# Two chunks of attention output, in two of four groups, turned by DMA instead of TensorE

## Chip, cores and metric

The kernel runs on one core of one Trainium2 chip. The metric is the device time of one execution in microseconds (us), taken as the median of several runs.

## What is computed

```python
xn = layernorm(x)                      # x: 1 x 2048 x 640, fp32
q, k, v = split(xn @ wqkv)             # 32 heads of 20
a = softmax over 8 keys at distance 0, 2, ..., 14 behind each token
s = (a applied to v) @ wo              # sliding dilated attention, then the output projection
h = silu(xn @ w1) @ w2                 # 640 -> 1536 -> 640
out = x + s * silu(h)
```

## The kernel before

**Groups and phases.** The 2048 tokens are cut into four groups of 512 (two halves of the sequence, and in each the even and the odd tokens, so that a distance of 2 becomes 1). Each group runs two phases on TensorE: QKV (`qkv_phase`, four quarters `q` of eight heads, each 5 x 4 x 3 matmuls of 480 columns) and FFN (`ffn_phase`: twelve blocks of w1 in `up`, twelve of w2 in `down`, and the output projection `wo_phase` of the group before). fp32 is carried as two fp32r parts, a high and a low one, and each product is three matmuls (high x high, low x high, high x low). VectorE does the attention of a group (`score`, `weigh`, `total`, `value`) while TensorE is in the FFN of the same group and at the start of the next QKV. The result goes into `O` (tokens on partitions, 640 columns), quarter by quarter; some of the last additions are done by GpSimd (lines 772 and 774), the others by VectorE.

**Turning.** TensorE needs the channels on partitions, so `O` and the normalised `x` are turned in five chunks of 128 columns. On TensorE that is `split_t` (line 620): four transposes of 128 x 128 against an identity (line 626) into one of two PSUM banks `rot`, a copy by ScalarE to the high part (line 630) and a subtraction by VectorE for the low part (line 636). `o_chunk` does that for `O`, called from QKV of the next group at the five places of `O_AT` (line 946: after the weights of chunk 2 or 4 in quarter 1, 2 or 3). Most of `x` is turned by DMA instead (`X_DMA`, `turn_x`, line 651): ScalarE packs the fp32 values into two planes of 16 bits (line 656), SyncE issues one DMA transpose for each plane (line 660), ScalarE puts the planes together again (line 665) and copies the high part (line 670), and VectorE subtracts (line 671).

**Buffers.** `OH`/`OL` and `TH`/`TL` are the same storage, 16 columns apart: in a slot lies first the turned `x` of a group, and, once its last w1 block is done, the turned `O` of that group, which `wo_phase` of the next FFN reads. `KV[q]` holds keys and values of a quarter, with a halo that DMAs fill (lines 693, 703 and 705); its key half is scratch for `value` (`partial`). Weights go through a ring of seven buffers `WR`; from the second or third use on they are loaded again by GpSimd's DMA queue (line 562), one load each time TensorE frees a buffer.

**Order.** Nothing is issued in the order in which the Python code names it. Every operation is added to a planner (`Weave`) with an engine, a duration, keys that it reads and writes, a priority, perhaps an earliest time `at`; `order` simulates the engines and fixes one order for each, and `plan` adds edges that close gaps on TensorE in that simulation. On the chip each engine runs its list in order and waits at the head of it. A small `prio` goes first. `spans` are ranges of `O` or `XIN` that wait for one another even where their columns differ.

Of the kernel before, what the change touches and what calls it, by code (L numbers as in the profile page):

```python
# [10 lines left out]
U16 = mybir.dt.uint16  # L11
AF = mybir.ActivationFunctionType
# [3 lines left out]
P = 128  # L16
# [5 lines left out]
CQ = HQ * DH  # L22
J = 8
T = 4
TOK = T * P
# [28 lines left out]
CARRY_AT = 8.0  # L54
X_SINGLE = (1,2,)
X_DMA = {1: (0, 1, 2, 3, 4), 2: (2, 3, 4)}
X_BY = {1: 2, 3: 0, 4: 1}
SLOW, ISSUE, SUB_LATE = 8, 2.0, 3
PACE0, PACE = -20.0, 12.0
BACK = {1: 0.0, 2: 40.0}  # L60
# [260 lines left out]
def local_attention_silu_ffn(ctx: ExitStack, tc: tile.TileContext, x, wqkv, wo, w1, w2, out):  # L321
    nc = tc.nc
# [18 lines left out]
    NG = len(groups)  # L341
# [15 lines left out]
    TH = [sb.tile([P, DC * TOK + OAT], F32R, name="th0")]  # L357
# [4 lines left out]
    TL = tiles("tl", 2, [P, DC * TOK + 64], F32R)  # L362
    chunks = lambda tiles, at: [v[:, at:at + DC * TOK].rearrange("p (c n) -> p c n", c=DC) for v in tiles]
    OH, OL = chunks(TH, OAT), chunks(TL, OAT)
    TH, TL = chunks(TH, 0), chunks(TL, 0)
# [6 lines left out]
    KV = tiles("kv", NQ, [P, 2, HALO + T, CQ])  # L372
    Q = tiles("q", NQ, [P, T, CQ])
    E = [v[:, :, CQ - W * HQ:].rearrange("p t (w h) -> p t w h", w=W) for v in Q]
    O = sb.tile([P, T, D], F32, name="o")
    PR = sb.tile([P, 2, W, CQ], F32, name="pr")
    L = tiles("l", 2, [P, T, W, HQ])
    XIN = sb.tile([P, T, D], F32, name="xin")
    G = sb.tile([P, T, D], F32, name="gate")
# [3 lines left out]
    TURN = sb.tile([P, TOK], F32, name="turn")  # L383
# [29 lines left out]
    def act(n, fn, reads, writes, prio, table=None, more=0.0, late=0.0, at=0.0, spans=()):  # L413
        return add("ACT", ac(n) + more, fn, reads, writes, prio, table=table, late=late, at=at, spans=spans)

    def free_for(old, new):

        add("DVE", 0.0, lambda: None, [], list(old) + list(new), 0)
# [8 lines left out]
    clock = [0.0]  # L427
# [214 lines left out]
    def both(k):  # L642
        return [k + (0,), k + (1,)]

    def chunk_span(of, c, write=False):
        return [(of, c * P, (T - 1) * D + (c + 1) * P, write)]

    def piece(tile_of, k):
        return tile_of.rearrange("p t d -> p (t d)")[:, k * TOK:(k + 1) * TOK]

    def turn_x(c, i, at, back):

        keys = [("xin", t) for t in range(T)]
        (a, ka), (b, kb) = (piece(G, X_BY[c]), ("buf", X_BY[c])) if c in X_BY else (TURN, ("turn",)), (piece(G, c), ("buf", c))
        into = XIN[:, :, c * P:(c + 1) * P]
        act(2 * TOK, lambda: nc.scalar.activation(
            a.bitcast(U16).rearrange("p (h t n) -> p h t n", h=2, t=T), into.bitcast(U16).rearrange("p t (n h) -> p h t n", h=2),
            AF.Copy), keys, both(ka), 150, at=at, spans=chunk_span("x", c))
        for h in range(2):
            dma(lambda h=h: nc.sync.dma_start_transpose(  # L660
                b.bitcast(U16).rearrange("p (h t n) -> p h t n", h=2, t=T)[:, h],
                a.bitcast(U16).rearrange("p (h n) -> p h n", h=2)[:, h]),
                [ka + (h,)], [kb + (h,)], P * TOK * 6, clock[0], ISSUE, SLOW)
        kh, kl = t_keys(i, [c], kinds=["th"]), t_keys(i, [c], kinds=["tl"])
        act(2 * TOK, lambda: nc.scalar.activation(
            into.bitcast(U16).rearrange("p t (n h) -> p h t n", h=2),
            b.bitcast(U16).rearrange("p (h t n) -> p h t n", h=2, t=T), AF.Copy),
            both(kb) + keys, [("xw", c)], 150, more=0.3, at=back, spans=chunk_span("x", c, True))
        hi, lo = (v[i][:, c, :].rearrange("p (t n) -> p t n", t=T) for v in (TH, TL))
        act(TOK, lambda: nc.scalar.activation(hi, into, AF.Copy), [("xw", c)] + keys, kh, 0)  # L670
        dve(TOK, lambda: nc.vector.tensor_tensor(out=lo, in0=into, in1=hi.bitcast(F32), op=OP.subtract),
            [("xw", c)] + keys + kh, kl, 0, lock=True, late=SUB_LATE, spans=chunk_span("x", c))

    def tile_spans(of, cs, ts):
        return [(of, t * D + c * P, t * D + (c + 1) * P, False) for t in ts for c in cs]
# [32 lines left out]
    def halo_keys(q):  # L708
        return [("halo", q, 1, 0), ("halo", q, 1, 112), ("halo", q, 2, 0), ("halo", q, 2, 112), ("halo", q, 3, 0),
                ("halo", q, 4, 0)] + [("kv", q, t) for t in range(T)]  # L710
# [93 lines left out]
    def o_chunk(g, c, i):  # L804
        qs = range(c * P // CQ, ((c + 1) * P - 1) // CQ + 1)
        split_t(O, [("o", q, t) for q in qs for t in (0, 2)], c, i, (OH, OL))
# [104 lines left out]
    def qkv_phase(g, i, io):  # L911
        for q in range(NQ):
            if g == 0 and q == 0:
                ps = first_quarter(i)
            else:
                ps = [bank() for t in range(T)]
                for c in range(DC):
                    wh, wl, kh, kl = w_next("q", q, c)
                    for t in range(T):
                        o, kp = ps[t]  # L920

                        def unit(c=c, t=t, o=trio_sums(o), wh=wh, wl=wl):
                            hi, lo = TH[i][:, c, tsl(t)], TL[i][:, c, tsl(t)]
                            vh, vl = trio(wh), trio(wl)
                            nc.tensor.matmul(o, hi, vh, start=c == 0, stop=False)  # L925
                            nc.tensor.matmul(o, lo, vh, start=False, stop=False)  # L926
                            nc.tensor.matmul(o, hi, vl, start=False, stop=c == DC - 1)  # L927
                        pe(3 * mm(3 * CQ), unit, t_keys(i, [c], [t]) + [kh, kl], [kp])
                    w_done()
                    if g:  # L930
                        for k in O_AT.get((q, c), ()):
                            o_chunk(g - 1, k, io)
            if groups[g][0] == 0:
                zero = KV[q][0:2, 0:2 - g, 0:HALO, :]
                add("POOL", 2.0 - g, lambda zero=zero: nc.gpsimd.memset(zero, 0.0), [] if g or not q else ["first"],
                    [("halo", q, 1, 0), ("halo", q, 2, 0), ("halo", q, 3, 0), ("halo", q, 4, 0)], clock[0] if g else 1 + 12 * q)
            for t in range(T):
                evac_qkv(g, q, t, *ps[t])
            halo(g, q)
            attend(g, q)  # L940
        attend(g, NQ)

    def t_keys(i, cs, ts=range(T), kinds=("th", "tl")):
        return [(k, i, c, t) for k in kinds for c in cs for t in ts]
# [37 lines left out]
    def gate(ts, cs):  # L982
        return of(G[:, ts.start] if ts.stop - ts.start == 1 else G[:, ts], cs)

    def gkeys(ts, cs):
        return [("g", t, cs.start) for t in range(ts.start, ts.stop)]
# [158 lines left out]
    def ffn_phase(g, i, ix, io):  # L1145
        if g + 1 < NG:
            behind = [("kv", XQ, 0)] if g else []
            step = 1 if g in X_SINGLE else 2
            for t in range(0, T, step):
                load_x(g + 1, t, step, behind=behind)  # L1150
            for t in range(T):
                ln_stats(t)
            ln_rstd(0, T)
            for t in range(T):
                ln_apply(t)
        ps = None
        by_dma = X_DMA.get(g, ())
        bufs = [("buf", c, h) for c in range(DC) for h in range(2)]
        for kind, f in plan(g):
            if kind == "w1":  # L1160
                up(g, i, f, io)
            elif kind == "wo":
                wo_phase(g - 1, io)
                if g == NG - 1:
                    free_for([("xin", t) for t in range(T)], [("xin", t, c) for t in range(T) for c in (0, CA)])
                for c in range(DC) if by_dma else ():
                    ts = slice(c * TOK // D, ((c + 1) * TOK - 1) // D + 1)
                    free_for(gkeys(ts, slice(0, CA)) + gkeys(ts, slice(CA, D)), bufs[2 * c:2 * c + 2])
                for k, c in enumerate(by_dma):
                    turn_x(c, ix, clock[0] + PACE0 + PACE * k, clock[0] + BACK[g])  # L1170
            elif kind == "x":
                if f not in by_dma:
                    split_t(XIN, [("xin", t) for t in range(T)], f, ix, (TH, TL), XIN[:, :, tsl(f)])
            elif kind == "o":
                o_chunk(g, f, io)
            elif kind == "rest":
                o_rest(g, f, io)
            else:
                ps = ps or tm_banks()
                down(f, ps)  # L1180
        for p, kp, ts, cs in tm_views(ps):
            n = (ts.stop - ts.start) * (cs.stop - cs.start)
            act(n, lambda p=p, ts=ts, cs=cs: nc.scalar.activation(gate(ts, cs), p, AF.Silu), [kp], gkeys(ts, cs) + bufs * bool(by_dma), 0, "silu")

    add("POOL", 0.7, consts, [], ["consts"], 0)
    act(1, lambda: nc.scalar.activation(SD[:, 1, 0:1], epst, AF.Sqrt), ["consts"], [("rs", 0)], 0, "sqrt")
# [37 lines left out]
```

## Time and profile before

| what | value |
|---|---|
| time, median of 3 runs (lowest, highest) | 602.38 us (601.88, 603.2) |
| the profiled execution | 600.52 us |
| its span, first to last instruction | 598.7 us |
| TensorE busy | 593.2 us, 99% |
| VectorE, ScalarE, GpSimd busy | 515.6, 236.9 and 163.5 us |
| granted TensorE clock, mean | 1.000 |

A matmul's duration in the profile runs from its start to its modelled end, and the next one starts before that end; so durations of TensorE add up to more than the busy time. The chain of waits that ended last shows each piece only for the time by which it moved the end. QKV of the four groups starts at about 7, 139, 284 and 431 us.

### The profile page before, as it was taken

To read this page: it belongs to the slowest core of one execution; us is meant where nothing else is said; L and a number is where in the kernel's file an instruction comes from. 1 tells how busy PE (TensorE), PEld (TensorE's weight loads), DVE (VectorE), ACT (ScalarE), POOL (GpSimd) and SP (SyncE) were. 2 spreads that over 40 slices of the span, in tenths; PEclk is the share of its full clock that TensorE was granted. 3 is DMA by queue.
4 is the path that set the end of the run, shared out by engine and by line. 5 is a ranking of instruction groups with operands and counts; after the bars stand their busy time and mean duration, and the time that the engine had idled before them with its cause. 6 is when DMAs were issued, how large, how long until landed. Compare 5 with 4: busy or idle time off the path is not lost.

```text
span 598.7 us, 9085 instructions
## 1 busy us (share of the span) xinstructions
PE 593.2 (99%) x3463; PEld 558.4 (93%) x3463; DVE 515.6 (86%) x505; ACT 236.9 (40%) x434; POOL 163.5 (27%) x229
## 2 busy tenths in 40 slices
PE   8999999999999999999999999999999999999997
PEld 7999999999999999999999999999999999999997
DVE  6599999999799978999979999999828799999544
ACT  5447364453546224555324604452412342313230
POOL 5800102233110153433211137433122133441100
PEclk9999999999999999999999999999999999999999
DMA  9999999779999999965699999997689997766652
GB/s 295 305 315 335 323 409 387 299 244 299 275 330 313 324 256 334 250 211 164 184 336 293 308 360 269 274 265 223 211 219 284 295 332 247 242 193 215 198 181 88
DMA packets 74823, 162.90 MB, mean 272 GB/s; under 512 B 14509, under 2 KB 38797, under 8 KB 74781
## 3 DMA queue, kind: packets, MB, share of 16 engines
q1 hardware_dynamic: 54941, 82.62, 47.4%
q0 software_dynamic: 19296, 79.31, 44.5%
q8 instruction: 27, 0.44, 0.3%
q10 hardware_dynamic: 544, 0.41, 0.2%
q14 instruction: 15, 0.12, 0.1%
HBM read 107.91 MB, written 34.16 MB: 237 GB/s over the span
## 4 chain that ended last, share of the span: by engine, by line
PE 98%; DMA 1%; DVE 0%; issue 0%
PE acc L969 22%; PE acc L971 15%; PE acc L925 10%; PE acc L926 10%; PE acc L927 10%; PE rot L1104 9%; PE rot L1106 9%; PE rot L1105 9%; PE acc L875 2%; PE rot L626 2%; DMA xin<-in_A_x_dram 1%; PE rot L859 0%; PE rot L1087 0%; DVE st L844 0%; PE rot L818 0%; DVE gate L1055 0%
## 5 line engine op out<-in xcount | busy, mean ns | idle before, releaser
L925 PE MATMUL acc<-w,th 128*128 128x480 f32 x300 | 110.8, 369 | 0.0
L926 PE MATMUL acc<-w,tl 128*128 128x480 f32 x300 | 109.8, 366 | 0.0
L927 PE MATMUL acc<-w,th 128*128 128x480 f32 x300 | 109.8, 366 | 0.0
L969 PE MATMUL acc<-w,sh 128*128 128x384 f32 x384 | 108.6, 328 | 0.0
L719 DVE TENSOR_TENSOR pr<-q,kv 128x2560 f32<-128x2560 f32 x32 | 90.2, 2819 | 18.1 <-ACT th L630 13.0
L971 PE MATMUL acc<-w,sh 128*128 128x256 f32 x384 | 104.7, 273 | 0.0
L1104 PE MATMUL rot<-th,w 128*128 128x512 f32 x240 | 92.1, 384 | 0.0
L761 DVE TENSOR_TENSOR pr<-q,kv 128x2560 f32<-128x2560 f32 x32 | 90.7, 2834 | 1.1
L1105 PE MATMUL rot<-tl,w 128*128 128x512 f32 x240 | 91.0, 379 | 0.0
L1106 PE MATMUL rot<-th,w 128*128 128x512 f32 x240 | 91.0, 379 | 0.0
L722 DVE TENSOR_REDUCE l<-pr 128x128 f32<-128x2560 f32 x32 | 89.6, 2801 | 0.2
L1117 ACT ACTIVATE sh<-rot 128x512 fp32r<-128x512 f32 x48 | 28.8, 599 | 138.5 <-PE rot L1106 138.4
L562 POOL DMA_DIRECT2D w<-half_w x72 | 38.8, 539 | 156.5 <-PE acc L971 56.8
L971 PEld LDWEIGHTS acc<-w,sh 128*128 128x128 f32 x384 | 73.7, 192 | 0.6
L969 PEld LDWEIGHTS acc<-w,sh 128*128 128x128 f32 x384 | 72.6, 189 | 0.6
L562 POOL DMA_DIRECT2D w<-half_q x52 | 27.8, 535 | 122.9 <-PE acc L927 75.4
L927 PEld LDWEIGHTS acc<-w,th 128*128 128x128 f32 x300 | 56.7, 189 | 4.0
L926 PEld LDWEIGHTS acc<-w,tl 128*128 128x128 f32 x300 | 56.7, 189 | 3.8
L925 PEld LDWEIGHTS acc<-w,th 128*128 128x128 f32 x300 | 56.7, 189 | 3.8
L969 PE MATMUL acc<-w,sl 128*128 128x384 f32 x192 | 55.9, 328 | 0.0
L1119 DVE TENSOR_TENSOR sl<-sf,sh 128x512 fp32r<-128x512 f32 x48 | 42.0, 876 | 14.3 <-ACT sf L1118 14.1
L971 PE MATMUL acc<-w,sl 128*128 128x256 f32 x192 | 52.3, 273 | 0.0
(106 smaller groups left out, 1059.9 us busy)
## 6 DMA issues: line engine op xcount, KB each, us to landing
w<-half_w POOLq DMA_DIRECT2D x72, 640.0 KB, 5.5
w<-half_q POOLq DMA_DIRECT2D x52, 480.0 KB, 4.9
half_w<-w SPq DMA_DIRECT2D x24, 640.0 KB, 6.2
half_q<-w SPq DMA_DIRECT2D x20, 480.0 KB, 6.7
kv<-kv SPq DMA_DIRECT2D x15, 560.0 KB, 8.1
w<-half_wo POOLq DMA_DIRECT2D x10, 640.0 KB, 7.0
kv<-kv SPq DMA_DIRECT2D x15, 420.0 KB, 8.3
gate<-in_B_w_dram SPq DMA_DIRECT2D x16, 320.0 KB, 6.9
```

The costliest lines, as they stand in the source:

```text
L562: add("POOL", 1.0, lambda: nc.gpsimd.dma_start(both, src), [("half", u)], [kh, kl], due + 10, nbytes=2 * n * P * 4)
L719: dve(2560, lambda: nc.vector.tensor_tensor(out=PR, in0=win(qq[:, t:t + 2, :], W, 0), in1=win(kv[:, 0, t:t + 2, :], W, CQ), op=OP.mult), h ...
L722: dve(2560, lambda: nc.vector.tensor_reduce(out=l[:, t:t + 2].rearrange("p t w h -> p (t w h)"), in_=PR.rearrange("p t w (h d) -> p (t w h ...
L761: dve(2560, lambda: nc.vector.tensor_tensor(out=PR.rearrange("p t w (h d) -> p t (w h) d", d=DH), in0=e[:, t:t + 2].rearrange("p t w h -> ...
L925: nc.tensor.matmul(o, hi, vh, start=c == 0, stop=False)
L926: nc.tensor.matmul(o, lo, vh, start=False, stop=False)
L927: nc.tensor.matmul(o, hi, vl, start=False, stop=c == DC - 1)
L969: nc.tensor.matmul(a[t][0][:, :CA].rearrange("p (m h) -> p m h", h=2), st, col_a(w), start=first, stop=last)
L971: nc.tensor.matmul(b[t // 2][0][:, h * CB:(h + 1) * CB].rearrange("p (m h) -> p m h", h=2), st, col_b(w), start=first and h == 0, stop=las ...
L1104: nc.tensor.matmul(to, wh[:, cs], hi, start=c == 0, stop=False)
L1105: nc.tensor.matmul(to, wh[:, cs], lo, start=False, stop=False)
L1106: nc.tensor.matmul(to, wl[:, cs], hi, start=False, stop=c == DC - 1)
```

## The change

In the second and third group (g = 1, 2) chunks 0 and 1 of `O` are no longer turned by `o_chunk` in QKV of the next group. `turn_os`, called at the end of `ffn_phase`, gives them the way of `turn_x`: ScalarE packs into two 16-bit planes, two DMA transposes on SyncE's queue, ScalarE unpacks and copies the high part, VectorE subtracts. The planes lie in the key halves of `KV[0]` and `KV[1]` (`spare`), which are lent for that time (`lend`). The earliest times given to the planner are 35 and 55 us after the start of that FFN for the two packs and 80 and 82 us for the two unpacks. `turn_x` is split into `send` and `join`, with the same steps as before.

```diff
@@ -54,6 +54,9 @@
 CARRY_AT = 8.0
 X_SINGLE = (1,2,)
 X_DMA = {1: (0, 1, 2, 3, 4), 2: (2, 3, 4)}
+O_DMA = {1: (0, 1), 2: (0, 1)}
+O_OUT = (), (35.0, 55.0), (35.0, 55.0), (10.0, 25.0)
+O_BACK = (), (80.0, 82.0), (80.0, 82.0), (40.0, 55.0)
 X_BY = {1: 2, 3: 0, 4: 1}
 SLOW, ISSUE, SUB_LATE = 8, 2.0, 3
 PACE0, PACE = -20.0, 12.0
@@ -648,28 +651,60 @@
     def piece(tile_of, k):
         return tile_of.rearrange("p t d -> p (t d)")[:, k * TOK:(k + 1) * TOK]
 
-    def turn_x(c, i, at, back):
-
-        keys = [("xin", t) for t in range(T)]
-        (a, ka), (b, kb) = (piece(G, X_BY[c]), ("buf", X_BY[c])) if c in X_BY else (TURN, ("turn",)), (piece(G, c), ("buf", c))
-        into = XIN[:, :, c * P:(c + 1) * P]
+    def send(src, c, keys, of, by, to, at):
+
+        (a, ka), (b, kb) = by, to
         act(2 * TOK, lambda: nc.scalar.activation(
-            a.bitcast(U16).rearrange("p (h t n) -> p h t n", h=2, t=T), into.bitcast(U16).rearrange("p t (n h) -> p h t n", h=2),
-            AF.Copy), keys, both(ka), 150, at=at, spans=chunk_span("x", c))
+            a.bitcast(U16).rearrange("p (h t n) -> p h t n", h=2, t=T),
+            src[:, :, c * P:(c + 1) * P].bitcast(U16).rearrange("p t (n h) -> p h t n", h=2),
+            AF.Copy), keys, both(ka), 150, at=at, spans=chunk_span(of, c))
         for h in range(2):
             dma(lambda h=h: nc.sync.dma_start_transpose(
                 b.bitcast(U16).rearrange("p (h t n) -> p h t n", h=2, t=T)[:, h],
                 a.bitcast(U16).rearrange("p (h n) -> p h n", h=2)[:, h]),
-                [ka + (h,)], [kb + (h,)], P * TOK * 6, clock[0], ISSUE, SLOW)
-        kh, kl = t_keys(i, [c], kinds=["th"]), t_keys(i, [c], kinds=["tl"])
+                [ka + (h,)], [kb + (h,)], P * TOK * 6, at + 2, ISSUE, SLOW)
+
+    def join(to, into, kinto, reads, c, i, dest, at, spans=((), ())):
+
+        b, kb = to
         act(2 * TOK, lambda: nc.scalar.activation(
             into.bitcast(U16).rearrange("p t (n h) -> p h t n", h=2),
             b.bitcast(U16).rearrange("p (h t n) -> p h t n", h=2, t=T), AF.Copy),
-            both(kb) + keys, [("xw", c)], 150, more=0.3, at=back, spans=chunk_span("x", c, True))
-        hi, lo = (v[i][:, c, :].rearrange("p (t n) -> p t n", t=T) for v in (TH, TL))
-        act(TOK, lambda: nc.scalar.activation(hi, into, AF.Copy), [("xw", c)] + keys, kh, 0)
+            both(kb) + reads, kinto, 150, more=0.3, at=at, spans=spans[0])
+        kh, kl = t_keys(i, [c], kinds=["th"]), t_keys(i, [c], kinds=["tl"])
+        hi, lo = (v[i][:, c, :].rearrange("p (t n) -> p t n", t=T) for v in dest)
+        act(TOK, lambda: nc.scalar.activation(hi, into, AF.Copy), kinto + reads, kh, 0)
         dve(TOK, lambda: nc.vector.tensor_tensor(out=lo, in0=into, in1=hi.bitcast(F32), op=OP.subtract),
-            [("xw", c)] + keys + kh, kl, 0, lock=True, late=SUB_LATE, spans=chunk_span("x", c))
+            kinto + reads + kh, kl, 0, lock=True, late=SUB_LATE, spans=spans[1])
+
+    def turn_x(c, i, by, to, at, back):
+        keys = [("xin", t) for t in range(T)]
+        send(XIN, c, keys, "x", by, to, at)
+        join(to, XIN[:, :, c * P:(c + 1) * P], [("xw", c)], keys, c, i, (TH, TL), back,
+             (chunk_span("x", c, True), chunk_span("x", c)))
+
+    def turn_o(c, i, by, to, at, back):
+        qs = range(c * P // CQ, ((c + 1) * P - 1) // CQ + 1)
+        send(O, c, [("o", q, t) for q in qs for t in (0, 2)], "o", by, to, at)
+        join(to, by[0].rearrange("p (t n) -> p t n", t=T), both(by[1]), [], c, i, (OH, OL), back)
+
+    def turn_os(g, i, begun):
+        by_dma = O_DMA.get(g, ())
+        for c in by_dma:
+            lend(c)
+        for k, c in enumerate(by_dma):
+            turn_o(c, i, spare(c, 0), spare(c, 1), begun + O_OUT[g][k], begun + O_BACK[g][k])
+        for c in by_dma:
+            lend(c, True)
+
+    def spare(q, k):
+
+        return KV[q][:, 0].rearrange("p t m -> p (t m)")[:, k * TOK:(k + 1) * TOK], ("spare", q, k)
+
+    def lend(q, back=False):
+        old = [(k, q, t) for k in ("kv", "own", "val") for t in range(T)] + [("partial", q)] + halo_keys(q)
+        new = [k for p in range(2) for k in both(("spare", q, p))]
+        free_for(*((new, old) if back else (old, new)))
 
     def tile_spans(of, cs, ts):
         return [(of, t * D + c * P, t * D + (c + 1) * P, False) for t in ts for c in cs]
@@ -929,7 +964,8 @@
                     w_done()
                     if g:
                         for k in O_AT.get((q, c), ()):
-                            o_chunk(g - 1, k, io)
+                            if k not in O_DMA.get(g - 1, ()):
+                                o_chunk(g - 1, k, io)
             if groups[g][0] == 0:
                 zero = KV[q][0:2, 0:2 - g, 0:HALO, :]
                 add("POOL", 2.0 - g, lambda zero=zero: nc.gpsimd.memset(zero, 0.0), [] if g or not q else ["first"],
@@ -1154,6 +1190,7 @@
             for t in range(T):
                 ln_apply(t)
         ps = None
+        begun = clock[0]
         by_dma = X_DMA.get(g, ())
         bufs = [("buf", c, h) for c in range(DC) for h in range(2)]
         for kind, f in plan(g):
@@ -1162,17 +1199,21 @@
             elif kind == "wo":
                 wo_phase(g - 1, io)
                 if g == NG - 1:
+                    turn_os(g, io, begun)
+                if g == NG - 1:
                     free_for([("xin", t) for t in range(T)], [("xin", t, c) for t in range(T) for c in (0, CA)])
                 for c in range(DC) if by_dma else ():
                     ts = slice(c * TOK // D, ((c + 1) * TOK - 1) // D + 1)
                     free_for(gkeys(ts, slice(0, CA)) + gkeys(ts, slice(CA, D)), bufs[2 * c:2 * c + 2])
                 for k, c in enumerate(by_dma):
-                    turn_x(c, ix, clock[0] + PACE0 + PACE * k, clock[0] + BACK[g])
+                    by = (piece(G, X_BY[c]), ("buf", X_BY[c])) if c in X_BY else (TURN, ("turn",))
+                    turn_x(c, ix, by, (piece(G, c), ("buf", c)), clock[0] + PACE0 + PACE * k, clock[0] + BACK[g])
             elif kind == "x":
                 if f not in by_dma:
                     split_t(XIN, [("xin", t) for t in range(T)], f, ix, (TH, TL), XIN[:, :, tsl(f)])
             elif kind == "o":
-                o_chunk(g, f, io)
+                if f not in O_DMA.get(g, ()):
+                    o_chunk(g, f, io)
             elif kind == "rest":
                 o_rest(g, f, io)
             else:
@@ -1181,6 +1222,8 @@
         for p, kp, ts, cs in tm_views(ps):
             n = (ts.stop - ts.start) * (cs.stop - cs.start)
             act(n, lambda p=p, ts=ts, cs=cs: nc.scalar.activation(gate(ts, cs), p, AF.Silu), [kp], gkeys(ts, cs) + bufs * bool(by_dma), 0, "silu")
+        if g < NG - 1:
+            turn_os(g, i, begun)
 
     add("POOL", 0.7, consts, [], ["consts"], 0)
     act(1, lambda: nc.scalar.activation(SD[:, 1, 0:1], epst, AF.Sqrt), ["consts"], [("rs", 0)], 0, "sqrt")
```

## Rows read from the trace of the kernel before

**Rows 1.** The page: busy time by engine, and the chain that ended last by engine.
```profile
PE 593.2 (99%) x3463; PEld 558.4 (93%) x3463; DVE 515.6 (86%) x505; ACT 236.9 (40%) x434; POOL 163.5 (27%) x229
...
PE 98%; DMA 1%; DVE 0%; issue 0%
```

**Rows 2.** TensorE's waits, all of them: us in total, times, longest.
```profile
PE rot L831 <- POOL ident masks.py:199: 1.4, 1, 1.4
PE rot L859 <- DVE xin L849: 0.2, 1, 0.2
```

**Rows 3.** Instructions by line and shape, TensorE's turning of O: busy us, mean ns.
```profile
L626 PE MATMUL rot<-ident,o 128*128 128x128 f32 x72 | 10.8, 273 | 0.0
```

**Rows 4.** The chain that ended last in time order, turning: start, us moved.
```profile
158.05 0.44 PE rot L626 x4
...
303.63 0.44 PE rot L626 x4
...
367.73 0.44 PE rot L626 x4
...
384.45 0.44 PE rot L626 x4
...
450.08 0.44 PE rot L626 x4
...
567.71 0.44 PE rot L818 x4
```

**Rows 5.** Instructions by line and shape, ScalarE and VectorE in both ways of turning.
```profile
L630 ACT ACTIVATE th<-rot 128x512 fp32r<-128x512 f32 x25 | 14.9, 596 | 57.8 <-PE rot L626 57.8
...
L636 DVE TENSOR_TENSOR tl<-rot,th 128x512 fp32r<-128x512 f32 x18 | 12.4, 687 | 4.4 <-ACT th L630 4.4
...
L665 ACT ACTIVATE xin<-gate 128x1024 uint16<-128x1024 uint16 x8 | 10.9, 1366 | 0.0
...
L671 DVE TENSOR_TENSOR tl<-xin,th 128x512 fp32r<-128x512 f32 x8 | 6.0, 744 | 0.0
...
L656 ACT ACTIVATE gate<-xin 128x1024 uint16<-128x1024 uint16 x5 | 5.2, 1050 | 2.7 <-POOL xr L1018 2.7
L670 ACT ACTIVATE th<-xin 128x512 fp32r<-128x512 f32 x8 | 5.1, 632 | 0.3
```

**Rows 6.** Line 660, the DMA transposes on SyncE's queue: issue min/median/max ns, landing.
```profile
L660 SPq DMA_TRANSPOSE gate<-gate x10: 1212/1303/1564, 219.1 to 389.5; - x10
...
DMA to landing us min/median/max: 6.0/7.2/8.5
```

**Rows 7.** GpSimd in order of time, FFN of the second and third group.
```profile
267.23 0.86 POOL L774 TENSOR_TENSOR o<-kv 128x320 f32<-128x320 f32 x1
268.04 0.57 POOL L562 DMA_DIRECT2D w<-half_q x1
271.17 0.53 POOL L562 DMA_DIRECT2D w<-half_q x1 [2.56 <-PE rot L1106]
...
398.37 0.87 POOL L774 TENSOR_TENSOR o<-kv 128x320 f32<-128x320 f32 x1
```

**Rows 8.** ScalarE in order of time, end of the second group's FFN, start of QKV.
```profile
274.36 0.60 ACT L1117 ACTIVATE sh<-rot 128x512 fp32r<-128x512 f32 x1 [0.22 <-PE rot L1106]
...
281.65 0.49 ACT L1183 ACTIVATE gate<-acc 128x384 f32<-128x384 f32 x1 [6.20 <-PE acc L969]
...
284.18 0.98 ACT L1183 ACTIVATE gate<-acc 128x384 f32<-128x384 f32 x2 [0.34 <-PE acc L969]
...
294.61 0.44 ACT L680 ACTIVATE kv<-acc 128x320 f32<-128x320 f32 x1 [2.72 <-PE acc L927]
```

**Rows 9.** The chain that ended last: the last matmul of the second group's FFN.
```profile
284.08 0.11 PE acc L971
```

**Rows 10.** Line 562, the weight loads of 236 to 300 us: issue to landing.
```profile
DMA to landing us min/median/max: 3.5/4.0/7.4
```

**Rows 11.** VectorE in order of time, the last additions into O of the last group.
```profile
562.45 0.48 DVE L774 TENSOR_TENSOR o<-pr 128x320 f32<-128x320 f32 x1
```

## The prediction

> **What bounds the kernel now.** First the page: TensorE is busy for 593.2 of 598.7 us, no other engine for more than 515.6, and the chain that ended last is 98% TensorE [rows 1]. A busy engine could still be one that is fed late, so next its waits: there are two, 1.4 and 0.2 us, both at lines 831 and 859 in the first quarter [rows 2]. From then on TensorE runs from one instruction into the next. So the span is the sum of what TensorE is given, and work taken from it shortens the span unless it creates a wait, of which there is none to trade against.
>
> What one turning is worth I read in the chain in order of time. Each `split_t` moves the end by 0.44 us there, for four transposes [rows 4]. A second reading needs no modelled end: chunk 0 of `O` is turned at the same place of three QKV phases, at 158.05, 303.63 and 450.08 [rows 4]. The first period is 145.58 us, the second 146.45. TensorE has the same work in both, but that the second has two `x` chunks on TensorE (367.73 and 384.45 [rows 4]) and the first none. The difference is 0.87 us, 0.435 for one turning. This also shows that five chunks turned by DMA in the first of these periods cost TensorE nothing.
>
> **The change, part by part.**
>
> *Removed from TensorE.* Two chunks in each of two groups: 4 turnings, 16 of the 72 transposes of this line [rows 3]. 4 x 0.435 = 1.74 us. The mean duration of a transpose is 273 ns [rows 3], which would make 16 x 0.273 = 4.4 us; four in a row then would take 1.09 us, where the chain has 0.44. I take 1.74, because both readings of the end agree on it, and keep 4.4 as a bound. The Trainium skill goes by the duration too: "TensorE: Matmul & The Clock Gate", Part 4, gives about 275 ns for a transpose inside a kernel; by it the sum would be 16 x 0.275, an estimate of 4.4 us. The trace has the same duration, and a pitch of 0.11 us, which decides here.
>
> *ScalarE.* It loses 4 copies of 0.596 and gets 4 packs of 1.050, 4 unpacks of 1.366 and 4 copies of 0.632 [rows 5]: 12.2 - 2.4 = 9.8 us more, on 236.9 [rows 1]. That is nothing in the sum as long as nothing that TensorE awaits stands behind them. These are the silus and, between FFN and QKV, the gates (line 1183), which empty the PSUM banks.
>
> *VectorE.* It loses 4 subtractions of 0.687 and gets 4 of 0.744 [rows 5]: 0.2 us, in the FFN instead of the next QKV. What is late next is seen at the end: the last addition into `O` ends at 562.93 [rows 11], and TensorE asks for the remaining chunks from 567.71 on [rows 4]. Arriving 1.74 us earlier, at 565.97, it still finds them done; so VectorE costs nothing.
>
> *SyncE and its queue.* 8 DMA transposes, issued in 1.2 to 1.6 us, landing 6.0 to 8.5 us after that [rows 6]: some 10 us of the queue. Behind them stand the carry loads (lines 703 and 705) for `KV[0]` and `KV[1]`, which must now wait until the lent halves are back; only the next group's `score` reads these, and for that the shifts of line 693 are needed too, which come after the evacuation at 294.61 [rows 8].
>
> *GpSimd.* A pack reads `O` over a range of all columns, so GpSimd's additions (line 774) can wait for it, and weight loads stand behind these in its order. Loads land after 7.4 us at worst in this stretch [rows 10]; they are some 3.1 us apart [rows 7], and with seven buffers one is issued about six units, 19 us, ahead of its use. A hold under 11 us costs nothing.
>
> *The lent keys.* The two chunks cannot be packed before quarters 0 and 1 are added up, whatever the earliest times of 35 and 55 us say. For the second group the second chunk is complete at 267.23 + 0.86 = 268.09, for the third at 399.24 [rows 7]. The high copies also wait for the last w1 block, whose silu starts at 274.36 [rows 8], since `OH` lies where `x` lay. `KV[0]` must be free when QKV evacuates its first quarter, at 294.61 [rows 8]. A pack, two issues and a landing (1.05 + 2 x 1.3 + 7.2) bring the second chunk to about 279, unpack and copy to 281; so the tight place is the second group. The third has 399.24 instead of 268.09 against a QKV one period later (146.45): 15 us more room.
>
> *The PSUM banks at that place.* The last FFN matmul is at 284.08 [rows 9], the gates run from 281.65 to 285.16 [rows 8]. QKV needs its fourth bank 3 x 3 x 0.2 = 1.8 us after it starts, at 286.0, and the fifth gate has emptied it by 284.7: 1.3 us to spare.
>
> A rule speaks against the change: the Trainium skill, "VectorE: DVE Perf Modes", The three transpose paths and Rules for kernel authors, says to use TensorE where PSUM will do as the destination, with 390 ns against 1309 for the DMA (128 x 128, two bytes). The trace agrees that the DMA takes longer, 7.2 us for a plane of four tiles [rows 6], and shows no TensorE wait behind 16 such transposes [rows 2]; by its figures the 32 tiles of 16 bits would take an estimate of 32 x 1.309 = 41.9 us if TensorE had to wait for them, against 1.74 taken from it. The trace has them beside the path, so the sum has nothing for them.
>
> Sum: 598.7 - 1.74 = 596.96 us of span; the profiled execution's 600.52 becomes 598.78. That execution lies 1.86 us under the median of the runs, 602.38; the same offset gives 600.64 for the median.
>
> **Rivals.**
>
> *Given back.* ScalarE comes to the unpack of the second chunk (second group) before the planes have landed, and the gates stand behind it. Against: 281 is before the first gate. For: at 268.09 ScalarE has silus and three `x` unpacks in hand, so the pack may start 2.5 us late, two slow issues take 3.1, a slow landing 8.5: 268.09 + 2.5 + 1.05 + 3.1 + 8.5 = 283.2, and with unpack and copy the gates begin at 285.2, 3.6 late. Less the 1.3 to spare TensorE waits 2.3 us: 602.9. Half of that delay gives a time around 601.5; I put 602.2 for this case.
>
> *Slower.* The same queue, but a wait that TensorE really pays: landing later than seen before. To end 0.2% above 602.38 the wait must be 1.74 + 1.2 = 2.9 us, so the gates 4.2 late, the landing at 283.9 or after; with the transposes 2 us slower than the slowest of the 16, from sharing the DMA engines with weight loads, the wait is 4.3 us and the time 604.9. Against it: 0.7 us past the worst row at every step. The simulated order can also put the unpack behind the gates, which ends this case.
>
> *More gained.* If a transpose holds TensorE for its duration, the time falls by 4.4 us to 598.0. The chain speaks against it. By the Trainium skill, "TensorE: Matmul & The Clock Gate", Part 4, this is the price.
>
> *It doesn't do what it says.* The chunks would still be turned by TensorE: 72 transposes, 602.4. The two tests on `O_DMA` exclude it; its chance is in the second case's.
>
> **How the numbers follow.** A measurement of this kernel can tell about 0.2%, 1.2 us, from no change. The forecast, 600.6, is 1.7 us below, not far beyond that. Chances: forecast 0.63, given back 0.22, slower 0.12, more gained 0.03. Of the forecast's part 0.04 goes to "same", since 0.5 us of wait or of spread is enough, and of the second case 0.02 falls on the fast side. Faster 0.64, same 0.24, slower 0.12. The range takes the lower end from the lowest run shown, 601.88 - 1.74 = 600.1, less 0.4 for a median of a few runs, 599.7; the upper end is the given-back case at its worst, 602.9. What is left out is the slower case and half of the gain by duration.
>
> **What would show it.** Right: line 626 with 56 transposes of `O`; both later QKV phases 0.87 us shorter; TensorE's waits still 1.6 us in all; line 660 with 24 issues. The forecast is wrong if TensorE has a new wait: at the start of the third QKV on the gates (given back, slower), at the second quarter's banks on line 680 (lent keys late), or on line 562 (GpSimd held). It is wrong in its price if TensorE waits for nothing and the phases shrink by another amount.

## The result, and the profile after

The changed kernel is slower: 603.99 us (median of 21 runs, 601.47 to 613.13) against 601.61 (21 runs, 600.26 to 603.2), a ratio of 1.0043 with a 95% interval of 1.0027 to 1.0059. Ratios leave out executions more than 1.5% above the fastest of their kernel, here the one of 613.13 us. The profiled execution took 603.26 us where that of before took 600.52, so 2.74 us are to be found.

First the page of the changed kernel, to be read beside [rows 1]: busy time, the clock in 40 slices, the chain by engine.

```profile
PE 593.4 (99%) x3447; PEld 557.9 (93%) x3447; DVE 515.2 (86%) x505; ACT 246.0 (41%) x442; POOL 164.1 (27%) x229
...
PEclk9999999999999999999999999999999989999999
...
PE 82%; DMA 8%; DVE 6%; issue 2%; ACT 1%; SPq 1%; POOL 0%; DVEq 0%; POOLq 0%; ACTq 0%
```

TensorE has 16 instructions fewer and is as long busy; one slice has a granted clock under 0.9; and the chain leaves TensorE for 18% of the span, against 2% before. Then the parts of the change, by line and shape (the turning on TensorE is line 629 now, and packs, unpacks and subtractions of the turned `O` are those with `kv`):

```profile
L629 PE MATMUL rot<-ident,o 128*128 128x128 f32 x56 | 8.4, 273 | 0.0
...
L670 ACT ACTIVATE kv<-kv 128x1024 uint16<-128x1024 uint16 x4 | 5.5, 1370 | 0.0
...
L657 ACT ACTIVATE kv<-o 128x1024 uint16<-128x1024 uint16 x4 | 4.2, 1054 | 0.0
...
L677 DVE TENSOR_TENSOR tl<-kv,th 128x512 fp32r<-128x512 f32 x4 | 2.7, 686 | 0.0
```

The 16 transposes are gone ([rows 3] had 72), and the added work has the sizes foreseen to within 0.06 us ([rows 5]). Now TensorE's waits, all of them, beside [rows 2]:

```profile
PE rot L1140 <- DVE tl L639: 2.2, 1, 2.2
PE rot L866 <- POOL ident masks.py:199: 1.4, 1, 1.4
PE rot L894 <- DVE xin L884: 0.5, 1, 0.5
```

The first is new: the first w1 matmul of the last group (line 1140) waits for a subtraction of `split_t` (line 639). TensorE in order of time at that place: start, duration.

```profile
479.44 0.60 PE L629 MATMUL rot<-ident,o 128*128 128x128 f32 x4
482.23 0.48 PE L1140 MATMUL rot<-th,w 128*128 128x512 f32 x1 [2.19 <-DVE tl L639]
...
483.41 0.63 PE L1141 MATMUL rot<-tl,w 128*128 128x512 f32 x1
...
486.61 0.38 PE L1140 MATMUL rot<-th,w 128*128 128x512 f32 x1
```

The last turning takes 0.44 us, so w1 could start at 479.88 and starts at 482.23, 2.35 late. Then its matmuls last 0.63 us instead of 0.38. By stretch of time (length, busy, matmuls, granted clock, DMA share, GB/s):

```profile
479.80:482.20 2.40, 0.24 (x3) 1.00 1.17 383
482.20:486.40 4.20, 4.17 (x12) 0.59 1.08 276
486.40:490.00 3.60, 3.60 (x26) 1.00 1.24 270
```

The clock falls from 2.4 to 1.2 GHz behind the wait and is back some 4 us later. This w1 block, 15 matmuls, takes 5.03 us, from 482.23 to 487.26; at 0.216 us each it takes 3.24. So the books are: minus 1.74, plus 2.35 of wait, plus 1.79 of half clock, plus 0.3 at 389.3 (a w2 matmul waits for a VectorE instruction behind an attention product that took 4.46 us instead of 2.82 while GpSimd added beside it; too short against the modelled ends to be among the waits listed), plus 0.05 at the start: 2.75 of the 2.74.

The other executions were not profiled, but the mean granted clock of each is on record, and 4.2 us at 0.59 take 0.3% off a mean of 1.000. Nine of the 21 have 0.997, like the profiled one, and a median of 604.0 us; eight have 0.999 or 1.000 and a median of 602.4; the other four have 0.994 or less and took 606.2 to 613.13. By the books the wait without the half clock gives 601.61 - 1.74 + 2.35 = 602.2, and with it 604.0. That fits a half clock behind the wait in some executions and none in others; where those that were not profiled lost theirs is not shown.

**Why VectorE is late there.** VectorE in order of time, kernel before, then the changed kernel. The subtraction for chunk 3 is line 636 before and 639 changed. The score of the last group's quarter 1 is line 719 before and 754 changed: the first of them in each list is for the first half of the tokens, the second for the second half.

```profile
468.30 2.83 DVE L719 TENSOR_TENSOR pr<-q,kv 128x2560 f32<-128x2560 f32 x1 [3.48 <-DMA kv<-kv]
...
478.72 1.49 DVE L767 TENSOR_TENSOR kv<-pr 128x1280 f32<-128x1280 f32 x1
480.13 0.68 DVE L636 TENSOR_TENSOR tl<-rot,th 128x512 fp32r<-128x512 f32 x1
480.73 2.81 DVE L719 TENSOR_TENSOR pr<-q,kv 128x2560 f32<-128x2560 f32 x1
```

```profile
466.92 2.83 DVE L754 TENSOR_TENSOR pr<-q,kv 128x2560 f32<-128x2560 f32 x1 [3.60 <-ACT q L717]
...
477.22 1.49 DVE L802 TENSOR_TENSOR kv<-pr 128x1280 f32<-128x1280 f32 x1
478.75 2.82 DVE L754 TENSOR_TENSOR pr<-q,kv 128x2560 f32<-128x2560 f32 x1
481.49 0.68 DVE L639 TENSOR_TENSOR tl<-rot,th 128x512 fp32r<-128x512 f32 x1
```

The two have changed places. There are two `rot` banks; chunk 3 lies in the one that the first w1 block needs next, and it is free only after that subtraction. TensorE at that place in the kernel before:

```profile
480.83 0.60 PE L626 MATMUL rot<-ident,o 128*128 128x128 f32 x4
481.19 0.46 PE L1104 MATMUL rot<-th,w 128*128 128x512 f32 x1
```

Before, the subtraction ended at 480.8 and the first w1 matmul started at 481.2: 0.4 us to spare, under a TensorE that showed no wait. Why the planner changed the order is read in its own simulated times:

```
                              before     changed
VectorE is free               478.35     475.28
chunk 3 can be subtracted     477.87     476.11
so it starts first            line 636   line 754 (2.81 us)
subtraction ends, simulated   479.03     478.77
first w1 block, simulated     482.32     480.56
quarter 1's first score       464.62     463.30    (on the chip 468.30 and 466.92)
```

On paper the new order has 1.8 us to spare. On the chip the first score of quarter 1 is 3.7 and 3.6 us behind paper, in both kernels alike. In the kernel before the profile names the halo copies of its keys (`kv<-kv`) as what that score waits for. In the changed kernel it names an evacuation by ScalarE, but one of quarter 2, which this score does not read, so the halo is the likely cause there too; the planner experiment below tests it.

### The profile page after: what moved, and what is told of

Read it like the earlier page. It is cut to its first block, busy times and chain, and to the rows that moved or that the text cites. A ratio compares the mean times of both kernels' runs of the same rounds, so it can differ in the third digit from the quotient of the medians.

```text
span 601.5 us, 9070 instructions
## 1 busy us (share of the span) xinstructions
PE 593.4 (99%) x3447; PEld 557.9 (93%) x3447; DVE 515.2 (86%) x505; ACT 246.0 (41%) x442; POOL 164.1 (27%) x229
## 4 chain that ended last, share of the span: by engine, by line
PE 82%; DMA 8%; DVE 6%; issue 2%; ACT 1%; SPq 1%; POOL 0%; DVEq 0%; POOLq 0%; ACTq 0%
PE acc L1005 19%; PE acc L1007 12%; PE acc L960 8%; PE acc L962 8%; PE acc L961 8%; PE rot L1140 8%; PE rot L1141 8%; PE rot L1142 8%; DMA half_wo<-w 4%; DMA kv<-kv 3%; DVE pr L754 2%; PE acc L910 2%; DVE l L757 1%; PE rot L629 1%; DMA pr<-in_A_wqkv_dram 1%
## 5 line engine op out<-in xcount | busy, mean ns | idle before, releaser
L754 DVE TENSOR_TENSOR pr<-q,kv 128x2560 f32<-128x2560 f32 x32 | 91.9, 2871 | 17.9 <-DMA kv<-kv 13.9
L796 DVE TENSOR_TENSOR pr<-q,kv 128x2560 f32<-128x2560 f32 x32 | 91.0, 2845 | 0.9
L1155 DVE TENSOR_TENSOR sl<-sf,sh 128x512 fp32r<-128x512 f32 x48 | 40.0, 834 | 19.9 <-ACT sf L1154 19.8
L1140 PEld LDWEIGHTS rot<-th,w 128*128 128x128 f32 x240 | 45.7, 190 | 8.4 <-DVE tl L639 2.4
```

What stands on the lines that cost most here:

```text
L754: dve(2560, lambda: nc.vector.tensor_tensor(out=PR, in0=win(qq[:, t:t + 2, :], W, 0), in1=win(kv[:, 0, t:t + 2, :], W, CQ), op=OP.mult), h ...
L796: dve(2560, lambda: nc.vector.tensor_tensor(out=PR.rearrange("p t w (h d) -> p t (w h) d", d=DH), in0=e[:, t:t + 2].rearrange("p t w h -> ...
L1140: nc.tensor.matmul(to, wh[:, cs], hi, start=c == 0, stop=False)
```

## Experiments

**One swap in the changed kernel.**

```diff
-        for o in self.plan():
+        done = self.plan()
+        a, b = self.swap
+        done.remove(b)
+        done.insert(done.index(a) + 1, b)
+        for o in done:
             o.fn()
...
+    wv.swap = subs[2, 3], scores[3, 1, 2]
```

`a` is the subtraction of chunk 3, `b` the score of the last group; the lines left out keep the two operations under these names.

> The changed kernel with one VectorE instruction moved: the score of the last group (quarter 1, second half of the tokens, 2.8 us) goes behind the subtraction of turned chunk 3, not ahead of it. Theory A (the order on VectorE holds the PSUM bank that the first w1 block of the last group needs): the subtraction ends near 479.4, TensorE comes at 479.9, the wait of 2.2 us at line 1140 and the stretch of half clock behind it are gone; about 4.1 us less than the changed kernel, near 600.1 where the kernel before has 601.6. Rival B (the eight more DMA transposes delay the halo copies and so the whole of VectorE): the wait stays, 603 to 604.

601.51 us (12 runs) against 601.57, ratio 1.0008 (0.9994 to 1.0022). Its waits of TensorE, and VectorE where one of them arises:

```profile
PE acc L1012 <- DVE gate L1045: 0.8, 2, 0.6
PE rot L1145 <- DVE tl L643: 0.4, 1, 0.4
```

```profile
503.71 2.82 DVE L758 TENSOR_TENSOR pr<-q,kv 128x2560 f32<-128x2560 f32 x1
506.45 3.14 DVE L1045 TENSOR_TENSOR gate<-acc,gate 128x384 f32<-128x384 f32 x6
```

The wait of 2.2 us is 0.4, the clock behind it stays at 1.00, and by the medians 2.5 us of the loss are gone. Not the 4.1 I expected: the next place where VectorE is late shows, the gate products behind a score, whose banks w2 needs.

**The same swap, the other way, in the kernel before.** Edit as above, with the score as `a` and the subtraction as `b`.

> The kernel before, all turning as it was, with the same two VectorE instructions the other way round: the subtraction of chunk 3 goes behind that score. Theory A: the subtraction ends near 483.6 where TensorE wants the bank at 481.4, so a wait of some 2.2 us at line 1104 and half clock after it, 1.8 us more: plus 4 us, near 605.6. Rival B: no more DMA than before, so no change, 601.6.

606.97 us (9 runs), ratio 1.0084 (1.0058 to 1.0111). Its longest wait, the only new one over 1 us, and VectorE there:

```profile
PE rot L1109 <- DVE tl L640: 5.5, 1, 5.5
```

```profile
472.33 2.83 DVE L723 TENSOR_TENSOR pr<-q,kv 128x2560 f32<-128x2560 f32 x1 [6.64 <-DMA kv<-kv]
...
484.28 2.82 DVE L723 TENSOR_TENSOR pr<-q,kv 128x2560 f32<-128x2560 f32 x1
487.02 0.68 DVE L640 TENSOR_TENSOR tl<-rot,th 128x512 fp32r<-128x512 f32 x1
```

With no DMA transpose added, exchanging two VectorE instructions costs more than the whole change. The profiled execution, 609.37 us, is the longest of the nine, and in it the wait is 5.5 us and not the 2.2 expected, because the halo copies let the first score start at 472.33, where the kernel before has 468.30; 0.8 us of that is TensorE's own delay. This landing differs between the two executions, and the new order passes that on to TensorE.

**Each group alone.** `O_DMA = {1: (0, 1)}`, and `O_DMA = {2: (0, 1)}`.

> Only the second group's two chunks go by DMA. Its order on VectorE has the subtraction of chunk 3 of the third group ahead of the score, as the kernel before. Theory A: two turnings less on TensorE, no wait, minus 0.87 us: near 600.7. Rival B: half of the DMA transposes, so about half of the loss: 602.5 to 603.

> Only the third group's two chunks go by DMA. Its order on VectorE has the score ahead of the subtraction, as the changed kernel. Theory A: minus 0.87 us for two turnings, plus 2.3 us of wait and 1.8 us of half clock: near 604.8, so at least as slow as the whole change. Rival B: as the second group alone, 602.5 to 603.

The second group alone: 601.05 us, ratio 0.9986 (0.9976 to 0.9996), so by the ratio 0.84 us less (0.2 to 1.4) where 0.87 were expected. The third alone: 602.9, ratio 1.0027 (1.0009 to 1.0044), by the ratio 1.6 us more where 3.2 were expected. The signs are those of the two orders on VectorE, and each has four of the eight added transposes, so the number of transposes is not the cause. The profile of the third group alone fell into an execution of 616.1 us, with the wait for line 639 in it at 3.6 us, and does not price a typical one. The mean clocks say more on the size that was missed: nine of its 13 executions have 0.999 or 1.000 and took 601.5 to 603.4 us, the three with 0.997 took 606.1 to 607.0. So, by the mean clock, few of them paid for a stretch of half clock.

**The planner told that the halo lands late.**

```diff
-                    quick=KEYS_IN * ((g, q) in KEYS_FIRST))
+                    quick=KEYS_IN * ((g, q) in KEYS_FIRST), more=3.5 * (g == NG - 1))
```

> The changed kernel, with the planner told that the halo copies of the last group land 3.5 us later than it had them. It now puts the subtraction of chunk 3 ahead of the score, and the six gate products of the output projection ahead of the next attention step. Theory A (the order was made for a VectorE that is 3.5 us earlier than the real one): no wait of TensorE over 0.5 us behind the first quarter, near 600.0 where the kernel before has 601.6 (ratio 0.997). Rival B (DMA load of the transposes): as the changed kernel, 603 to 604. Rival C (each new order only moves the wait to another place): a wait of 1 to 2 us elsewhere, 601 to 602, as with the one swap.

> The control: the kernel before, with the same 3.5 us told to the planner. If the gain of the run beside it comes from the turnings taken from TensorE, this stays at 601.6 (TensorE waited for nothing before, there is nothing to gain). If it comes from a better order, this gets faster as well.

With the change: 600.69 us (11 runs, the lowest 598.73) against 601.41, ratio 0.9983 (0.9959 to 1.0007). TensorE's waits are back to those of the first quarter, and VectorE has the subtraction ahead of the score and the gates ahead of the next step:

```profile
PE rot L866 <- POOL ident masks.py:199: 1.4, 1, 1.4
PE rot L894 <- DVE xin L884: 0.3, 1, 0.3
```

```profile
476.16 0.68 DVE L639 TENSOR_TENSOR tl<-rot,th 128x512 fp32r<-128x512 f32 x1
...
478.28 2.82 DVE L754 TENSOR_TENSOR pr<-q,kv 128x2560 f32<-128x2560 f32 x1
...
499.78 3.14 DVE L1040 TENSOR_TENSOR gate<-acc,gate 128x384 f32<-128x384 f32 x6
```

This profiled execution took 598.73 us, 1.79 under that of before: the 1.74 of the forecast, once nothing is given back. Seven of the 11 runs are at 598.7 to 600.7, near theory A's 600.0; the other four at 606.2 to 612.7. The interval takes in 1, so over all runs a gain is not shown; that the loss is gone from most of them is. The control without the change: 600.96, ratio 0.9993 (0.9984 to 1.0001), so the order by itself gains little or nothing.

**The bank freed by another engine.** The changed kernel with its order, but chunk 3 of the third group is copied out by ScalarE:

```diff
+        if whole is TURN:
+            act(TOK, lambda: nc.scalar.activation(TURN, ps, AF.Copy), [kp], both(("turn",)), 0)
+            dve(TOK, lambda: nc.vector.tensor_tensor(out=lo, in0=TURN, in1=hi.bitcast(F32), op=OP.subtract),
+                both(("turn",)) + kh, kl, 0, lock=True)
+            return
...
-        split_t(O, [("o", q, t) for q in qs for t in (0, 2)], c, i, (OH, OL))
+        split_t(O, [("o", q, t) for q in qs for t in (0, 2)], c, i, (OH, OL), TURN if (g, c) == (2, 3) else None)
```

> The changed kernel with the order on VectorE as it is (score ahead of the subtraction of chunk 3), but ScalarE copies the turned chunk into SBUF and VectorE subtracts from there, so that the PSUM bank is free without VectorE. Theory A: it is the bank, so the wait of 2.2 us at the first w1 block is gone; VectorE is as late as before, and the gate products may wait, 1 to 2 us: 601 to 602. If TensorE waited for the low half itself or for anything else of VectorE's, nothing changes: 604.

602.62 us (12 runs), ratio 1.0021 (0.9999 to 1.0043). The first w1 block starts at once, at 480.44, while the subtraction runs only at 484.44; the longest new wait is now at the gates:

```profile
PE acc L1010 <- DVE gate L1045: 2.0, 1, 2.0
```

```profile
481.70 2.83 DVE L759 TENSOR_TENSOR pr<-q,kv 128x2560 f32<-128x2560 f32 x1
484.44 0.68 DVE L636 TENSOR_TENSOR tl<-turn,th 128x512 fp32r<-128x512 f32 x1
```

So it was the bank, not the low half itself. And a VectorE that is late makes TensorE wait at the next thing that it owes. This execution, with the clock at 0.65 on average for 4.2 us behind the wait at the gates, took 604.61 us. The median is 0.6 us above the 601 to 602 expected, and the interval just takes in 1.

**The packs of O later.** `O_OUT` with (60.0, 62.0) in place of (35.0, 55.0): with the late halo in both groups, without it in both, and with it in the second group alone.

> The run with the late halo in the planner, and the two packs of O at 60 and 62 us instead of 35 and 55, so that the DMA transposes of chunk 0 stand behind those of the next group's x on SyncE's queue and not between them. Median as the run beside it, near 600.0. If the long times in the tail of the changed kernel (606 to 613) come from x planes that land late behind planes of O, the highest of these runs is lower, under 603; if they come from the DMA queue as such, the tail stays.

> The changed kernel with the packs of O at 60 and 62 us and nothing else; on VectorE the score still stands ahead of the subtraction of chunk 3. Theory A: the order on VectorE and the late planes are two separate losses; this one keeps the first, so a wait at the first w1 block of the last group and a median of 602.5 to 604, and loses the second, so no run over 605.5. If the late packs alone were what helped in the run with both, the median is 600.

> The late halo in the planner, and the packs at 60 and 62 us in the second group alone; in the third group the planes of chunk 0 stay ahead of those of x. The median is near 600.0 either way. If the long times come from the second group, no run over 603; if from the third, about one run in four is at 605 to 613, as with the packs early in both.

With the late halo: 599.63 us (12 runs, 598.75 to 602.61) against 601.41, ratio 0.9975 (0.9961 to 0.9989). This version beats the kernel before, and by the ratios the changed kernel too. Without it: 605.18 (6 runs), ratio 1.0072 (1.0049 to 1.0095), 1.2 us above the 602.5 to 604 expected, with this wait in the profile:

```profile
PE rot L1140 <- DVE tl L639: 2.3, 1, 2.3
```

In the second group alone: 600.22 (12 runs, the highest 604.32), ratio 0.9991 (0.9968 to 1.0014), which takes in 1. The order on VectorE is the larger loss and stays whatever the packs do. On the executions over 606 the runs do not agree: with the late halo and early packs they are 4 of 11, with late packs in both groups or in the second none of 24, but without the late halo 3 of 6 with late packs, where none was expected. And with late packs in the second group alone 4 of 12 are over 603, where either none or some over 605 were expected. What makes them is open.

The late packs open another wait, on ScalarE. The profile of the version with late halo and late packs in both groups is its longest execution, 602.61 us:

```profile
PE acc L960 <- ACT q L717: 1.6, 1, 1.6
```

```profile
321.77 0.89 DVE L607 BATCH_NORM_STATS2 st<-xin 128x6 f32<-128x320 f32 x2 [1.49 <-DMA xin<-in_A_x_dram]
```

```profile
322.93 0.30 ACT L613 ACTIVATE sd<-mv,epst 128x4 f32<-128x4 f32 x1 [12.53 <-DVE mv L609]
```

In this order a step of the layernorm (line 613) stands on ScalarE ahead of the evacuations of QKV's quarter 2 (line 717) and waits for the last part of the next group's `x` to land; TensorE waits for a bank, and behind that the clock is at 0.65 on average for 4.2 us. The changed kernel has the same order on ScalarE, but there this step starts at 318.80 and no wait shows; in the kernel before it stands behind the evacuations, at 324.10. The other two profiles with late packs have this wait with 0.5 and 0.8 us.

**What a long execution looks like.** The profile of the second group alone caught one, of 611.02 us. It is a single execution and explains no median. TensorE's longest wait, ScalarE, and SyncE's queue:

```profile
PE acc L960 <- ACT gate L1224: 6.0, 1, 6.0
```

```profile
287.88 1.34 ACT L670 ACTIVATE xin<-gate 128x1024 uint16<-128x1024 uint16 x1 [7.15 <-DMA gate<-gate]
...
289.79 2.59 ACT L1224 ACTIVATE gate<-acc 128x384 f32<-128x384 f32 x6
```

```profile
257.63 12.13 SPq L662 DMA_TRANSPOSE gate<-gate  x3
270.04 11.63 SPq L662 DMA_TRANSPOSE kv<-kv  x2
```

The issues of the transposes take up to 7 us instead of 1.3, an unpack of `x` stands at the head of ScalarE until its planes land, and the gates that free QKV's banks stand behind it. That is the queue of my two rivals, at the place I had named, with planes of `x` and not of `O`. What stretches the issues is open. It is not this queue alone: of the weight loads issued on GpSimd's queue from 245 to 300 us those of 480 KB landed after 15.0 us (median) in this execution, where the changed kernel's profile has 3.7.

## Why the prediction was wrong

- **What bounds it: right.** TensorE had no wait, and the end is its sum plus waits.
- **1.74 us for 16 transposes: right.** The second group alone gave 0.84 (0.2 to 1.4) for half of them, the run with the late halo 1.79 in its profile. The bound by duration, 4.4, half of which is 2.2, is refuted.
- **VectorE "costs nothing": the step that failed.** "What is late next is seen at the end", I wrote, and compared the last addition into `O` with the last turnings. I counted VectorE's work and looked at one deadline. The deadline that mattered was 86 us earlier, the `rot` bank at the first w1 block, and could be read beforehand: a subtraction that ends at 480.8 and a matmul that starts at 481.2. I also took VectorE's order as given. The change re-plans it, and the third group alone, 0.87 us less of TensorE's time in the last QKV, was enough to put a step of 2.8 us ahead of one of 0.7. What I had at nothing cost 2.35 us of wait in the profiled execution.
- **What I did not price: the clock.** In the profiled execution a wait of 2.35 us cost 4.1, since the clock fell behind it. Without that, by the books above, the median would be 602.2 and inside the range.
- **ScalarE, GpSimd, the lent keys, the tight gates: no cost in the profiled execution.** TensorE shows no wait at the gates and none for `KV[0]` or the weights. In the long execution above, of the second group alone, the gates made TensorE wait 6 us.
- **"Given back" and "slower".** Slower is what came, and not by the mechanism I gave a chance to: not planes that land late, but an evacuation queued behind attention. The upper end of the range, 602.9, rested on the one place where I had looked for a small margin. The 601.5 for half of that delay does not follow: half of 3.6 less the 1.3 to spare is 0.5 us of wait and gives 601.1, half of the wait gives 601.8. And the median that I started from, 602.38 of three runs, was 0.77 above that of 21.

## What to carry to other kernels

Where an engine without waits sets the time, list for each resource that it takes over (a PSUM bank above all) how long before its use the other engine lets go; the smallest of these margins, here 0.4 us, is what a change of order may spend. Where a planner makes the order, a saving on one engine re-deals the orders of all; compare its simulated times with the trace, and correct the one that is late before judging the change: with 3.5 us added to one landing most executions gained, and with the packs moved behind the other DMA transposes as well the change gained 0.25%.

## What was not expected of the hardware

The same wait can cost its length or nearly twice that: behind 2.35 us without matmuls the clock was at 0.59 on average for 4.2 us, behind 2.49 us at the same place (changed kernel with the packs later) it stayed at 1.00. Shorter waits elsewhere were followed by a slow clock too: 2.0 us at the gates (bank freed by ScalarE) and 1.6 us in QKV (late halo and late packs), each by 0.65 for 4.2 us. The halo copies of one place let the first score start at 468.30 in one execution and at 472.33 in another with the same work up to there, of which 0.8 is TensorE's delay; the order of before hid that and the new one did not.
